# Reordered order strings in a one-core attention and S4 kernel

## The chip, the core and the metric

The kernel runs on one core of a Trainium2 chip, in one launch. The core has five engines that run side by side, each with its own queue of instructions, taken in order: TensorE (PE, matrix multiplies; weight loads are listed as PEld), VectorE (DVE), ScalarE (ACT), GpSimd (POOL) and SyncE (SP, which here only issues DMA transfers). They work on SBUF and PSUM, the on-chip memories; PE writes only PSUM, and a PSUM tile must be read out ("evicted") by DVE or ACT before it can be used again. An instruction that needs another engine's result waits on a semaphore, and everything behind it in its own queue waits too. The metric is the time of one execution on the device in microseconds (us); lower is better.

## The reference

The input `x` has 2048 rows of 512 values in bfloat16. Four layers follow each other: attention (A), S4 convolution (B), A again, B again, each added to its layer-normalised input:

```python
x = A_x
x = x + _A_ref(_layernorm(x, axis=-1), A_wqkv, A_wo)
x = x + _B_ref(_layernorm(x, axis=-1), B_A_re, B_A_im, ...)
x = x + _A_ref(_layernorm(x, axis=-1), A_wqkv, A_wo)
x = x + _B_ref(_layernorm(x, axis=-1), B_A_re, B_A_im, ...)
```

A is sliding-window attention with 32 heads of width 16: row s sees the eight rows s, s−2, ..., s−14. Logits, softmax over the eight, a weighted sum of values and an output projection:

```python
idx = pos[:, None] - off[None, :]          # off = 0, 2, ..., 14
logits = jnp.einsum("bhsd,bhswd->bhsw", q, kg) * scale
attn = _softmax(jnp.where(mask, logits, -1e9), axis=-1)
o = jnp.einsum("bhsw,bhswd->bhsd", attn, vg)
```

B builds, for each of the 512 channels, a convolution kernel of length 2048 from 128 complex modes, `K = sum over n of C exp(dt A l) dt B`, transforms kernel and input with a Fourier transform of length 4096, multiplies, transforms back, and adds `u * Dskip`. The convolution kernel is the same in both B layers.

## The kernel before

Rows stand in 16 blocks of 128, so a block fills the 128 partitions. The work runs through these stages, in the order of time of the profile:

1. **Kernel generation** (`k_gen`, 0 to 107 us). Powers of the modes are built from squares (ACT, L1095, L1113, L1119) and products (DVE, L1099, L1102, L1127), and PE multiplies them into the convolution kernel (L1285). The front of the first attention (layer norm, transposes, projections) is woven in.
2. **First attention** (`LayerA.core`, about 107 to 182). Per quarter of four row blocks and feature tile, DVE multiplies queries with shifted keys (`mult`, L342, tile `prod`), PE sums over the head (`lsum`, L350), DVE takes a maximum (`mx`, L414), ACT exponentials (L430, L453), PE projects values (`v_proj`, L398, evicted at L400). Then, for each of the 16 row blocks, DVE multiplies attention with values (`pv_mult`, L472, tile `pav`), PE sums (L497), ACT evicts (L499) and PE projects out (L508), with ACT adding to x (L512, L514). Layer-norm statistics of the finished rows follow (ACT sums L145, DVE L170, L172, L177, L185, with a power function on POOL, L178, or on ACT, L155 and L156). The normalised rows are then written by DVE (L197) or ACT (L195).
3. **First convolution** (`FftB`, about 182 to 240). PE multiplies by transform matrices in two steps, for the kernel (`K`, then `k`) and for the input (`U`, then `u`). Each result passes PSUM and is evicted by ACT or DVE (`evac`, L810, or L877). DVE multiplies the spectra (`u_mult`, L865, tile `t`). The kernel's spectrum goes through DRAM (tile `kf_dram`) for use in the second convolution. The inverse transform has two steps: `i1` (L891, L895, tile `z`, evicted at L810), and the outputs (`i2` L919 to L926, `i2_cols` L940 to L945, tile `x_sb`). The second step uses the inverse twiddle matrices, `fb.g2` (tile `g_sb`, 1 MB, loaded by SP at L1499).
4. **Front of the second attention** (about 230 to 266), woven into the end of the convolution: layer norm (`h`, `a`, `p`, `n`), transposes on PE (`T`, L271) evicted to `xnT` (`E`, L273), key and query projections (`P`, L282, evicted at L285 to `kT_ext`; `Q`, L223, evicted at L225), and copies that extend the keys over block borders (`x`, `e`, L295).
5. **Second attention** to about 344, **second convolution** to the end, with the stored kernel spectrum read back.

What sets the order of the work is not a planner but strings in the source. For DVE, ACT, PE and SP a program issues the instructions in the order in which the characters of a string call the functions above, and each engine's queue gets its instructions in that order. There are seven:

- `ORDERK`: kernel generation and the front of the first attention.
- `CORE0`, `CORE1`: the two attention cores. `m` is a `prod` multiply, `l` its sum, `q` and `v` projections, `x` maximum, `e` exponentials, `r` reciprocal, `n` normalising of the attention weights, `T` its transposition, `P` and `S` (or `V`) the weighted sum, `O` output projection, `t` statistics, `b` and `d` the beginning and end of a layer norm, `a` and `f` its application to one row block, on DVE and ACT respectively.
- `ORDER0`, `ORDER1`: the two convolutions, with the letters above. `y` is `i1`, `w`, `v` and `z` are outputs; the letter A or D behind a token tells whether ACT or DVE evicts. `g` asks for the inverse twiddle.
- `ORDERF`: the front of the second attention.
- In `CORE1`, capital letters before the rest call the last parts of that front (`RKEYS` names them; `RROWS` gives the engine of each). `KROWS` gives the engine of the eight copies that permute the convolution kernel (L1468, tile `k_perm`).

How a string is run, here for the core:

```python
for c in "".join(order.split()):
    if c in ev:
        ev[c]()
    else:
        next(ops[c])()
```

The functions that the diff touches:

Of the kernel before, what the change touches and what calls it, by code (L numbers as in the profile page):

```python
# [21 lines left out]
S = 2048  # L22
# [20 lines left out]
DQT = 8  # L43
NQT = DQG // DQT
ORDERK = """
iCsCaibCiCbMsiGMisbisCMiibbCMsaiibcMTMMbcisGibbscbGMTibTiTsMbTbTciibTMasTaGcTGaGMaGaiiMMTGGGMlaG
MMsbTMlTWalayyiMaiMybysMiteMateMaMqMMMMaaMqikkQMMKMwMMkMqblMdMTHkqaKlaqQUWUqTaQlUTkkkKayqUUqaypp
aUxaUpyUyxUtkUtpadUeHlKUTTUqeqQkTxkaQKxUkTlkWqTqpK3Tlx3ypkxQTkTpEpyqyy3H3KqkttTQlekWkeTKxUkKUxTU
kkkKkTkUlkKzUzTUTqzUzpUpUUUtKxpeUtUqUExUQepkkUUxxkUKUpEpokxXkUKkoKkkxpKpZXoxXxZZ
"""  # L50
ORDER0 = """
g KD KA KA KA KA KD KD KA KA KD KA kD KA KD KA KD kA UA UD KA UD kA UD UA kD UA UD UA kA kD u kD u m
m u u kA kD u kD UA UA m UA m u UD u kD UA UA m m m u UA kA kD UA kA m kD kA u yD u u m YD u m m m
YA yA u u u m u YA w000A YA m m m yD YA YA yA yD yA w010D yA
"""
LATE0 = "a s t g r b m"
ORDERF = """
yD h01 yA YA v100A v101A h00 v110A v111A h10 a0 v103D p0 n0D v113A h11 z03A S a1 z12A T0 E01D E00A
p1 z02A n1G P02 H2 Q00 P01 T1 a2 E10A p2 P03 E11D P10 P00 n2G H3 P12 a3 T2 E20A p3 P13 E21D n3D P23
P11 P21 T3 E30D P20 E31D x1D P22  # L60
"""
ORDER1 = """
UD UA UA UD UA UD UA UD UA UA UD u UD u u UA m m m UA UD u u u m m m UA u m u u u m u m m u YD m m
YA YA u yA u YD m m u w001A m u YA YA m YA w000D yA yA w010D YA w011D yA yD yA yD yA v102D v100A
v112D v110D v113D v103D v101A v111A
"""

CORE0 = """
mmvvvvlcvvmvllxemvmqrlmcnvlcxqTqvlcvvmmevvvvPqlr1qlPmnql4VTmmqO3lxSPq62lOS57mPlePSmOrSlPnOSPO8xT
SPbeOSrOPSnOPSTOPP9SbdOSPfdOPSOSaaPPfOFSfAOSfabWWWWODtGtCEHfB  # L70
"""
CORE1 = """
DACBFGEJIvHmKmllLN0123qmvqvmlvqmllvvmxvvqlqmemlqrlmnvqTvxmevllvPqvvvmvmqPlrlnmxqqTmSleqSmlPrOSOP
PmSnOSPPTOlblSOSPOxSedPOOrPSbnSPfdPOSWWWWfPOSOPSfPOSafOSbPdOafaStatafOf
"""
ROWS0 = (0, 2, 1, 3, 4, 5, 6, 7, 8, 9, 10, 11, 12, 13, 14, 15)
ROWS1 = (0, 2, 1, 3, 4, 5, 6, 7, 8, 9, 10, 11, 12, 13, 14, 15)
# [1 line left out]
ENGK = dict(b="AAAAAAAAAAAAAAAAA", y="AAAAAAAAAAAA", z="AAAA", e="AAAAAAAA", K="AAAAAAAAAAAAAAAA", Q="AAAAAAAA", x="AAAAAAAAAAAAAAAA")  # L79
STATD = (3,)  # L80
RKEYS = "ABCDEFGHIJKLN"
RROWS = "AADDAADAAADDA"
KROWS = "DDDDDADD"
VROWS = (*range(0, 16, 2), *range(1, 16, 2))


# [1309 lines left out]
def kernel(  # L1396
# [69 lines left out]
    def k_part(h, j):  # L1466
        cp = nc.scalar.copy if KROWS[h * 4 + j] == "A" else nc.vector.tensor_copy
        cp(kp[:, h * 64 + j * 16:h * 64 + (j + 1) * 16, :, :],  # L1468
           krs[h][:, :, j * 64:(j + 1) * 64].rearrange("p a (q r) -> p q a r", r=4))
# [79 lines left out]
    def ring_loads(*ns):  # L1549
        for n in ns:  # L1550
# [6 lines left out]
            ("P", 3, 3), ("Q", 0, 3), ("e", 1), ("e", 2), ("e", 3))  # L1557
    for c, e, (op, *ix) in zip(RKEYS, RROWS, rest):
        ev[c] = lambda e=e, op=op, ix=ix: front[op](*ix, dict(A="act", D="dve")[e])
# [51 lines left out]
```

## Time and profile before

| what | us |
|---|---|
| median of 3 runs | 392.2 |
| runs | 392.21, 392.2, 390.96 |
| the profiled execution, whole | 390.13 |
| its span | 388.4 |
| DVE busy | 369.8 (95%) |
| ACT busy | 336.1 (87%) |
| PE busy | 319.6 (82%) |
| POOL busy | 68.2 (18%) |

The span runs from the first to the last instruction of the trace; some 1.7 us of the execution lie around it. Every number of a row or a stage below is from this one execution, which is 2.1 us shorter than the median of the runs. The granted TensorE clock was 1.00 throughout. In a row of the timeline, the first number is the start in us, the second the duration, then the engine, the line, the operation, the tile written and the tiles read; a bracket at the end tells how long the engine stood idle before it and for whom.

### The profile page before, as it was taken

The numbers are of one execution on the slowest core, as the hardware profiler recorded it, in microseconds if no ns is written. First come the engines' busy times: TensorE is split into PE (matmuls) and PEld (weight loads), VectorE is DVE, ScalarE is ACT, GpSimd is POOL, SyncE is SP. The second block draws the span as 40 slices with busy tenths as digits, with TensorE's granted clock in tenths as the row PEclk, the third lists the DMA queues.
The fourth block names the chain that finished last, engine by engine and source line by source line (L and its number), as shares of the span: only waits on it lengthen the run. The fifth ranks groups of instructions, "written<-read, shape, count | busy, mean of one in ns | idle before, by whom it ended". The sixth has DMA issues, their size and how long they took to land.

```text
span 388.4 us, 14497 instructions
## 1 busy us (share of the span) xinstructions
PE 319.6 (82%) x6312; PEld 219.9 (57%) x6361; DVE 369.8 (95%) x442; ACT 336.1 (87%) x578; POOL 68.2 (18%) x97
## 2 busy tenths in 40 slices
PE   3000178889999998999998999999999998987895
PEld 2000036557634455666887899553445666667895
DVE  6999999999999999999999989979999999989985
ACT  7999999898669799999999998865576779989994
POOL 9400990000190000301622200300000030000000
PEclk9999999999999999999999999999999999999999
DMA  7950730414026465477676734067303076504606
GB/s 202 403 176 17 84 78 2 109 28 98 14 71 189 123 190 146 117 211 236 216 285 236 273 112 111 3 238 251 95 0 95 5 230 210 164 5 123 208 25 196
DMA packets 68301, 54.15 MB, mean 139 GB/s; under 512 B 33545, under 2 KB 58670, under 8 KB 67982
## 3 DMA queue, kind: packets, MB, share of 16 engines
q1 hardware_dynamic: 66566, 48.70, 42.5%
q0 software_dynamic: 1664, 4.52, 3.2%
q8 instruction: 49, 0.80, 0.8%
q14 instruction: 14, 0.11, 0.1%
q10 hardware_dynamic: 8, 0.00, 0.0%
HBM read 30.15 MB, written 13.24 MB: 112 GB/s over the span
## 4 chain that ended last, share of the span: by engine, by line
PE 41%; ACT 17%; DVE 8%; issue 5%; DMA 1%; DVEq 0%; ACTq 0%
PE pq L398 7%; PE pq L223 5%; DVE pav L472 4%; PE pp L282 4%; ACT a1s L810 3%; ACT ub L877 3%; PE po L497 3%; PE L L350 3%; PE pq L508 2%; PE pb L891 2%; PE pb L821 2%; PE pb L895 2%; PE pb L940 2%; PE L L424 2%; PE pb L941 1%
## 5 line engine op out<-in xcount | busy, mean ns | idle before, releaser
L472 DVE TENSOR_TENSOR pav<-attn,v_ext 128x4096 bf16<-128x4096 bf16 (+1 forms) x34 | 72.1, 2158 | 0.0
L342 DVE TENSOR_TENSOR prod<-qT,kT_ext 128x4096 bf16<-128x4096 bf16 x29 | 65.6, 2287 | 1.6 <-ACT qT L225 0.5
L1213 PE MATMUL pt<-ident,x_blk 128*128 128x128 bf16 x64 | 6.0, 242 | 39.3 <-ACT x_blk L195 39.3
L1127 DVE TENSOR_TENSOR A_t<-A_t,pow_t 128x1024 bf16<-128x1024 bf16 (+4 forms) x46 | 37.9, 868 | 0.1
L497 PEld LDWEIGHTS <-pav 64*128 64x128 bf16 x1984 | 30.8, 95 | 11.7 <-DVE pav L472 4.3
L497 PE MATMUL po<-ident,pav 64*128 64x64 bf16 x1984 | 34.3, 190 | 0.2
L508 PE MATMUL pq<-wop,oT 128*128 128x512 bf16 x122 | 31.7, 379 | 3.0 <-issue 2.4
L877 ACT CAST ub<-pb 128x1024 bf16<-128x1024 f32 x32 | 31.7, 1116 | 0.0
L828 PE MATMUL pb<-a1s,w_sb 128*128 128x64 bf16 x768 | 27.7, 193 | 3.6 <-ACT a1s L810 1.9
L810 ACT CAST a1s<-pb 128x1024 bf16<-128x1024 f32 x30 | 29.4, 1054 | 1.4 <-PE pb L821 1.3
L398 PE MATMUL pq<-wv,xnT 128*128 128x512 bf16 x122 | 30.1, 379 | 0.3
L1223 PE MATMUL pp<-xnT,kT_ext 128*128 128x512 bf16 x89 | 25.0, 402 | 5.1 <-ACT xnT L1216 2.0
L400 ACT CAST v_ext<-pq 128x512 bf16<-128x512 f32 x32 | 18.8, 590 | 11.0 <-PE pq L398 11.0
L828 PEld LDWEIGHTS <-w_sb 128*128 128x128 bf16 x768 | 24.9, 98 | 6.0 <-issue 4.3
L1213 PEld LDWEIGHTS <-x_blk 128*128 128x128 bf16 x64 | 4.5, 108 | 40.8 <-ACT x_blk L195 40.1
L178 POOL TENSOR_TENSOR ln_rstd<-ln_rstd,ln_mh 128x4 f32<-128x4 f32 x2 | 6.0, 2984 | 108.7 <-DVE ln_rstd L177 66.1
L1285 PE MATMUL pk<-B_t,A_t 128*64 128x84 bf16 (+1 forms) x512 | 23.4, 201 | 0.7 <-DVE A_t L1127 0.7
L223 PE MATMUL pq<-xnT,kT_ext 128*128 128x512 bf16 x89 | 23.7, 380 | 0.3
L1285 PEld LDWEIGHTS <-A_t 128*64 128x64 bf16 (+1 forms) x512 | 21.5, 103 | 3.9 <-DVE A_t L1127 0.9
L810 DVE CAST a1s<-pb 128x1024 bf16<-128x1024 f32 x18 | 21.4, 1216 | 1.3 <-PE pb L821 1.0
L398 PEld LDWEIGHTS <-xnT 128*128 128x128 bf16 x128 | 12.0, 98 | 15.7 <-issue 2.3
L508 PEld LDWEIGHTS <-oT 128*128 128x128 bf16 x128 | 12.5, 98 | 12.4
(262 smaller groups left out, 896.8 us busy)
## 6 DMA issues: line engine op xcount, KB each, us to landing
w_sb<-w_dram SPq DMA_DIRECT2D x64, 128.0 KB, 3.1
w_dram<-xnT SPq DMA_DIRECT2D x1, 4096.0 KB
kf_ring<-kf_dram SPq DMA_DIRECT2D x13, 256.0 KB, 3.8
kf_ring<-kf_dram SPq DMA_DIRECT2D x26, 128.0 KB, 4.0
v_ext<-v_ext SPq DMA_DIRECT2D x4, 784.0 KB, 5.9
x_blk<-in_A_x_dram SPq DMA_DIRECT2D x4, 512.0 KB, 5.0
kT_ext<-in_A_wqkv_dram SPq DMA_DIRECT2D x4, 512.0 KB, 13.3
x_sb<-in_A_x_dram SPq DMA_DIRECT2D x4, 512.0 KB, 6.8
```

The costliest lines, as they stand in the source:

```text
L223: nc.tensor.matmul(pq[:], lhsT=self.wqk[:, dt, ft * P:(ft + 1) * P], rhs=self.xnT[:, dt, q * 512:(q + 1) * 512], start=(dt == 0), stop=(dt ...
L342: nc.vector.tensor_tensor(pr, self.qT[q][:, ft].unsqueeze(1).to_broadcast([P, W, 4, P]), kap, ALU.mult)
L398: nc.tensor.matmul(pp[:], lhsT=xnT[:, dt, a * P:(a + 1) * P], rhs=wv[:, dt, :], start=(dt == 0), stop=(dt == NDT - 1))
L472: nc.vector.tensor_tensor(pv[:, i], attn[:, n % 4].unsqueeze(2).to_broadcast([P, W, DH // parts, H]), vap, ALU.mult)
L497: nc.tensor.matmul(po[:, h, 0, i * nt + ft, :], lhsT=pvf[rows, i, w, ft * P:(ft + 1) * P], rhs=ident[rows, rows], start=(w == 0 and ft + i ...
L508: nc.tensor.matmul(pw[:], lhsT=oT[:, ftp, :], rhs=self.wo[:, ftp, :], start=False, stop=(ftp == NDT - 1))
L810: (self.nc.scalar.copy if eng == "act" else self.nc.vector.tensor_copy)(dst, src)
L828: nc.tensor.matmul(p2[:, j, :], lhsT=self.w2[:, ec * EC + j, :], rhs=a1s[:, ec * EC + j, :], start=True, stop=True)
L877: nc.scalar.copy(ub[:], p2)
L1127: return lambda: nc.vector.tensor_tensor(*args)
L1223: nc.tensor.matmul(pps[kind, b, ft][:], lhsT=la.wqk[:, dt, c:c + P], rhs=la.xnT[:, dt, b * 512:(b + 1) * 512], start=(dt == 0), stop=(dt = ...
L1285: nc.tensor.matmul(o, lhsT=lhs, rhs=Bt[:, ri, c * CH + ql].rearrange("p b g -> p (b g)"), start=(not half and j % 4 == 0 and ri == 0), sto ...
```

## The change

All seven strings are permuted: the same functions are called, at other places. A few letters change besides. In `CORE0` and in `CORE1` one `a` becomes an `f`. In `ORDER0` one `kA` becomes `kD`; the eight inverse-transform evictions of ACT and DVE (`YA`, `yA`, `YD`, `yD`) become 4, 6, 2, 1 where they were 5, 4, 1, 3; and `g` stands no longer at the head of the string but behind 42 other tokens, ahead of the third `m`. In `ORDERF`, `E20A` becomes `E20D`. In `RROWS` the entry of key L (an extension slice of the keys) goes from D to A, and in `KROWS` the entries of parts E and F change places. `ORDERK` and `ORDER1` hold the same letters as before, in another order.

```diff
 ORDERK = """
-iCsCaibCiCbMsiGMisbisCMiibbCMsaiibcMTMMbcisGibbscbGMTibTiTsMbTbTciibTMasTaGcTGaGMaGaiiMMTGGGMlaG
-MMsbTMlTWalayyiMaiMybysMiteMateMaMqMMMMaaMqikkQMMKMwMMkMqblMdMTHkqaKlaqQUWUqTaQlUTkkkKayqUUqaypp
-aUxaUpyUyxUtkUtpadUeHlKUTTUqeqQkTxkaQKxUkTlkWqTqpK3Tlx3ypkxQTkTpEpyqyy3H3KqkttTQlekWkeTKxUkKUxTU
-kkkKkTkUlkKzUzTUTqzUzpUpUUUtKxpeUtUqUExUQepkkUUxxkUKUpEpokxXkUKkoKkkxpKpZXoxXxZZ
+iCsbCiGsbCaiCiCisGbMisbCMibMMiMGisbTiGbsMbMciibsbbMiisTMbTiGiTbbGMccsTiTaGacGaMGMMiaTbaMMGMMaisl
+GMaiMlTWaTMibaMlwMMTyyyyaMMTMMtseMiateaMMbkqaMkMTqKMMqMQqMaqHUcUladUlQUUTqakWaUQalkUykKUkykkyyTt
+atKUqqeTaaUpapxKpkUUelUxaQkpkdlHUTKxT3qxqWkpKTx3QTlpypTx3Tqpk3qlTkyyTHyWQUtqUTtqKeEkUeQTlTkkzkUK
+UkzKTkKUzTkUzqUTkqtKUktkxpxQpEUexekKUkpxxUkEUkpUKUKkoUxUUkpxopkKkUXKUXpxopXZZxxZ
 """
 ORDER0 = """
-g KD KA KA KA KA KD KD KA KA KD KA kD KA KD KA KD kA UA UD KA UD kA UD UA kD UA UD UA kA kD u kD u m
-m u u kA kD u kD UA UA m UA m u UD u kD UA UA m m m u UA kA kD UA kA m kD kA u yD u u m YD u m m m
-YA yA u u u m u YA w000A YA m m m yD YA YA yA yD yA w010D yA
+KD KA KA KA KA KD KD KA KA KD KA kD kA kD KA KD KA UA KD UA UD KA UD UA kD UA UD UA kA kD u kD u kA
+m UA m u kD UA kD u UA g m UA u m UA UD UD u u m kD m m kA UA u u u kA m kD kA kD m yA u u m m YA YD
+m u yA u m u u m YA YA m m yA YD w000A YA yD yA yA w010D yA
 """
 ORDERF = """
-yD h01 yA YA v100A v101A h00 v110A v111A h10 a0 v103D p0 n0D v113A h11 z03A S a1 z12A T0 E01D E00A
-p1 z02A n1G P02 H2 Q00 P01 T1 a2 E10A p2 P03 E11D P10 P00 n2G H3 P12 a3 T2 E20A p3 P13 E21D n3D P23
-P11 P21 T3 E30D P20 E31D x1D P22
+yD yA YA v101A v100A v110A v113A h01 h00 h10 a0 p0 v103D v111A n0D z03A h11 a1 S z12A T0 E00A E01D
+p1 z02A n1G H2 Q00 a2 P02 P03 T1 E10A E11D p2 P01 P12 n2G P10 H3 P13 T2 a3 p3 P00 E21D P11 E20D P20
+n3D P21 T3 E30D P22 P23 x1D E31D
 """
 ORDER1 = """
-UD UA UA UD UA UD UA UD UA UA UD u UD u u UA m m m UA UD u u u m m m UA u m u u u m u m m u YD m m
-YA YA u yA u YD m m u w001A m u YA YA m YA w000D yA yA w010D YA w011D yA yD yA yD yA v102D v100A
+UD UA UA UD UA UD UA UD UA UA UD u UD u u m u m UA u m UA u m UA m UD u m m u m u u u m m u YA YD u
+YA yA m m YD m u m u m w001A u YA YA m YA w000D yA yA w010D YA w011D yA yD yA yD yA v102D v100A
 v112D v110D v113D v103D v101A v111A
 """
 
 CORE0 = """
-mmvvvvlcvvmvllxemvmqrlmcnvlcxqTqvlcvvmmevvvvPqlr1qlPmnql4VTmmqO3lxSPq62lOS57mPlePSmOrSlPnOSPO8xT
-SPbeOSrOPSnOPSTOPP9SbdOSPfdOPSOSaaPPfOFSfAOSfabWWWWODtGtCEHfB
+vvvmcvlmvvxlcmvelmqvrlcqmnqlmcTxvvlvmvvvmvvqePPl1qmrlnq4lV5mxTqmS3llP2OSP7mqOSeOlPPSr6OmnSOPlbxP
+TdSeOPfrSOPSnOS8TOPSbPAOPSPfW9OSPOSffPOdSEOSfFWBWCfHWDtOGabta
 """
 CORE1 = """
-DACBFGEJIvHmKmllLN0123qmvqmvlqmllvvmxvvqlqmemlqrlmnvqTvxmevllvPqvvvmvmqPlrlnmxqqTmSleqSmlPrOSOP
-PmSnOSPPTOlblSOSPOxSedPOOrPSbnSPfdPOSWWWWfPOSOPSfPOSafOSbPdOafaStatafOf
+CDABIEGFLHvmlKqN0123JmmvllmvqmvvllqvvvqmmxlmleqmqrlnmvqTxvvvePllvvqvvmPqrlnqmlmmTxqSllSmePOPqrSm
+nPOSlWOOSPblWTxPSedPWOrSfOPSfPOSOPSnOSPbOSPWdfOPaSPOSfbPdOaStfOfSfatafO
 """
...
-RROWS = "AADDAADAAADDA"
-KROWS = "DDDDDADD"
+RROWS = "AADDAADAAADAA"
+KROWS = "DDDDADDD"
```

More of the change, by code (lines that the diff above doesn't have):

```diff
@@ L68 @@
 CORE0 = """
-mmvvvvlcvvmvllxemvmqrlmcnvlcxqTqvlcvvmmevvvvPqlr1qlPmnql4VTmmqO3lxSPq62lOS57mPlePSmOrSlPnOSPO8xT
-SPbeOSrOPSnOPSTOPP9SbdOSPfdOPSOSaaPPfOFSfAOSfabWWWWODtGtCEHfB
+vvvmcvlmvvxlcmvelmqvrlcqmnqlmcTxvvlvmvvvmvvqePPl1qmrlnq4lV5mxTqmS3llP2OSP7mqOSeOlPPSr6OmnSOPlbxP
+TdSeOPfrSOPSnOS8TOPSbPAOPSPfW9OSPOSffPOdSEOSfFWBWCfHWDtOGabta
 """
 CORE1 = """
-DACBFGEJIvHmKmllLN0123qmvqvmlvqmllvvmxvvqlqmemlqrlmnvqTvxmevllvPqvvvmvmqPlrlnmxqqTmSleqSmlPrOSOP
-PmSnOSPPTOlblSOSPOxSedPOOrPSbnSPfdPOSWWWWfPOSOPSfPOSafOSbPdOafaStatafOf
+CDABIEGFLHvmlKqN0123JmmvllmvqmvvllqvvvqmmxlmleqmqrlnmvqTxvvvePllvvqvvmPqrlnqmlmmTxqSllSmePOPqrSm
+nPOSlWOOSPblWTxPSedPWOrSfOPSfPOSOPSnOSPbOSPWdfOPaSPOSfbPdOaStfOfSfatafO
 """
```

## The prediction

> **What bounds the kernel now.** I read the page's span, engine shares and end chain first, then busy time by stage, then what VectorE (DVE) waits for, then single rows where the diff moves something.
>
> ```profile
> span 388.4 us, 14497 instructions
> ...
> PE 319.6 (82%) x6312; PEld 219.9 (57%) x6361; DVE 369.8 (95%) x442; ACT 336.1 (87%) x578; POOL 68.2 (18%) x97
> ...
> PE 41%; ACT 17%; DVE 8%; issue 5%; DMA 1%; DVEq 0%; ACTq 0%
> ```
> ```profile
> 160.00:170.00 10.00, 9.52 (x286) 6.33 (x289) 9.90 (x9) 9.80 (x26) 1.97 (x1) 1.00 0.68 197
> 170.00:182.00 12.00, 11.35 (x311) 7.27 (x316) 11.90 (x21) 11.82 (x27) 0.00 (x0) 1.00 0.70 214
> ...
> 200.00:220.00 20.00, 17.16 (x506) 15.98 (x504) 20.00 (x19) 20.00 (x23) 5.56 (x11) 1.00 0.77 285
> ...
> 230.00:258.00 28.00, 27.89 (x372) 20.13 (x367) 24.90 (x68) 22.37 (x39) 3.50 (x4) 1.00 0.22 65
> 258.00:300.00 42.00, 41.53 (x365) 18.84 (x370) 40.87 (x24) 26.58 (x44) 0.00 (x0) 1.00 0.43 141
> ```
> ```profile
> DVE x_sb L943 <- PE pb L941: 1.8, 4, 0.8
> ...
> DVE xnT L273 <- PE pt L271: 1.3, 1, 1.3
> DVE z L810 <- PE pb L895: 1.1, 1, 1.1
> DVE a1s L810 <- PE pb L821: 1.0, 2, 0.8
> ...
> DVE kT_ext L295 <- ACT kT_ext L285: 0.9, 1, 0.9
> DVE ln_nb L185 <- ACT ln_rstd L156: 0.7, 2, 0.5
> DVE prod L342 <- ACT qT L225: 0.5, 1, 0.5
> ```
>
> In the second fence the columns after the window's length are busy time of PE, weight load, DVE, ACT and POOL, then clock, DMA share and GB/s. DVE is idle for only 388.4 − 369.8 = 18.6 us. In the first convolution (200 to 220) DVE and ACT are both busy all 20.00 us; in the front of the second attention (230 to 258) PE is full (27.89 of 28), and after it (258 to 300) PE and DVE together (41.53 and 40.87 of 42). The chain names PE most, but an order earns only where it fills a hole, and the holes are small: the waits of the third fence sum to 7.3 us, of which 1.8 (x_sb) lie in the last convolution's tail, whose tokens keep their order. So 5.5 us is the most that these waits can yield, and since most are waits on a full PE, I expect a fraction.
>
> **Work that changes engine.** These durations price it:
>
> ```profile
> L197 DVE TENSOR_SCALAR xnT<-x_sb,ln_rstd,ln_nb 128x512 bf16<-128x512 bf16 x11 | 4.3, 415 | 0.1
> ...
> L273 DVE COPY xnT<-pt 128x1024 bf16<-128x1024 bf16 x5 | 3.2, 662 | 1.3 <-PE pt L271 1.3
> ...
> L295 DVE COPY kT_ext<-kT_ext 128x508 bf16<-128x508 bf16 x4 | 1.1, 285 | 0.0
> ```
> ```profile
> L195 ACT ACTIVATE xnT<-x_sb,ln_nb,ln_rstd 128x512 bf16<-128x512 bf16 x13 | 10.6, 814 | 0.0
> ...
> L273 ACT COPY xnT<-pt 128x1024 bf16<-128x1024 bf16 x3 | 3.1, 1018 | 0.0
> ...
> L295 ACT COPY kT_ext<-kT_ext 128x508 bf16<-128x508 bf16 x4 | 2.5, 621 | 0.1
> ```
>
> Each attention core moves one normalisation from DVE to ACT (CORE0, CORE1: one `a` becomes `f`): DVE −2 × 0.415, ACT +2 × 0.814. `E20` goes ACT to DVE: DVE +0.662, ACT −1.018. The slice `L` goes DVE to ACT: −0.285, +0.621. In ORDER0 one `k` eviction goes to DVE and one inverse-transform eviction comes back: of like size, zero. The two swapped permuted copies are zero too. Sum: DVE −0.83 + 0.66 − 0.29 = −0.45 us, ACT +1.63 − 1.02 + 0.62 = +1.23 us over the span. That alone moves nothing by more than a tenth of a per cent; what counts is where the holes go. I therefore took the changed order of each engine and added up row durations of the same instructions, stage by stage, letting each wait for its producer.
>
> **Kernel generation, 0 to 107.** DVE is full here, and the new order separates some pairs in which a DVE instruction needs the one right before it.
>
> ```profile
> 46.09 0.68 DVE L1127 TENSOR_TENSOR B_t<-B_t 128x1024 bf16<-128x1024 bf16 x1
> 46.69 0.68 DVE L1127 TENSOR_TENSOR cm_t<-B_t 128x1024 bf16<-128x1024 bf16 x1
> ...
> 64.95 0.69 DVE L1127 TENSOR_TENSOR A_t<-A_t,A_t 128x1024 bf16<-128x1024 bf16 x1
> 65.67 1.23 DVE L1127 TENSOR_TENSOR A_t<-A_t,pow_t 128x2048 bf16<-128x2048 bf16 x1
> ...
> 107.24 2.29 DVE L342 TENSOR_TENSOR prod<-qT,kT_ext 128x4096 bf16<-128x4096 bf16 x1 [0.51 <-PE L L350]
> ```
>
> Independent neighbours overlap: 46.69 − 46.09 = 0.60 for an instruction of 0.68. A dependent pair does not: 65.67 − 64.95 = 0.72 for 0.69. That is some 0.11 us a pair, and of eight such pairs at L1127 four remain: −0.46. Against it, two of the new A_t/B_t positions come before ACT's squares are done, by 0.28 and 0.2 in my sums: +0.3 to +0.5, estimated. I take −0.2 (bounds −0.5 and +0.3). [...] The stage's end (prod at 107.24, waiting 0.51 for PE) has the same order of work ahead of it in both, so part of either sign can still disappear there.
>
> **First attention and the hand-over to the first convolution, 107 to 183.**
>
> ```profile
> L178 POOL TENSOR_TENSOR ln_rstd<-ln_rstd,ln_mh 128x4 f32<-128x4 f32 x2 | 6.0, 2984 | 108.7 <-DVE ln_rstd L177 66.1
> ```
> ```profile
> 154.91 1.20 DVE L414 TENSOR_REDUCE mx<-L 128x128 bf16<-128x1024 f32 x1
> ...
> 158.77 8.90 DVE L472 TENSOR_TENSOR pav<-attn,v_ext 128x4096 bf16<-128x4096 bf16 x4
> ```
> ```profile
> 182.31 2.84 ACT L810 CAST a1s<-pb 128x1024 bf16<-128x1024 f32 x3
> ```
>
> POOL's power of 2.98 us stands between L177 and ln_nb, and DVE goes on with other work meanwhile. Before, four multiplies (8.90 us) cover it; after, a maximum and one multiply, 1.20 + 8.90 / 4 = 3.4 us, so it is covered with 0.4 to spare and costs nothing. If that cover fails, DVE stands with all its multiplies queued behind ln_nb: up to 1 us, by the maximum's slot. The extra ACT normalisation falls at about 160, where ACT is idle only 0.20 + 0.18 us until 182 (second fence): 0.81 − 0.38 = 0.4 of it comes out late at ACT's first eviction (182.31). A variance step (L172) that moves up waits up to 0.5 for ACT's sums. DVE itself would arrive 0.35 earlier. PE and both evictors start the convolution together, so I charge the later one: +0.4, bounds −0.35 and +0.75.
>
> **First convolution, 182 to 240.** Both evictors are full, so a kf eviction or multiply earlier or later changes only who waits; ACT's and DVE's sums differ from before by under 0.15 us. The hole before the inverse transform (1.1 in the third fence) is DVE waiting for PE while ACT still has its queue of evictions; it shrinks only if ACT is earlier, and it isn't. I take −0.1, bounds −0.5 and +0.5. The load `g`:
>
> ```profile
> 183.96 1.54 SPq L1499 DMA_DIRECT2D g_sb<-g_dram  x1
> ...
> 200.07 5.82 SPq L853 DMA_DIRECT2D kf_nat<-kf_nat  x8
> ```
> ```profile
> g_sb<-g_dram SPq DMA_DIRECT2D x1, 1024.0 KB, 6.0
> ```
> ```profile
> 226.11 1.19 ACT L945 CAST x_sb<-pb 128x1024 bf16<-128x1024 f32 x1
> ```
>
> It is issued at 183.96 and lands 6.0 us later. After, it is issued by SP between the transfers around 205, behind which eight quarter swaps of 3.6 us are in line, and lands by 215 even if it takes 10; the first output that needs it is evicted at 226.11. SP has no other work there that DVE waits on within 5 us. Cost zero; if the swaps behind it are late by its whole 6.0 us, 1 us reaches DVE.
>
> **Front of the second attention, 240 to 266.**
>
> ```profile
> 254.30 1.29 DVE L273 COPY xnT<-pt 128x1024 bf16<-128x1024 bf16 x2 [1.27 <-PE pt L271]
> ...
> 257.09 1.23 DVE L295 COPY kT_ext<-kT_ext 128x2032 bf16<-128x2032 bf16 x3 [0.90 <-ACT kT_ext L285]
> 258.36 2.29 DVE L342 TENSOR_TENSOR prod<-qT,kT_ext 128x4096 bf16<-128x4096 bf16 x1
> ...
> 264.00 4.49 DVE L342 TENSOR_TENSOR prod<-qT,kT_ext 128x4096 bf16<-128x4096 bf16 x2 [0.55 <-ACT qT L225]
> ```
>
> The 1.27 stays: PE is full, and as many matmul groups stand ahead of the last transposition. Of the three extension copies that now follow it (1.23 together, 0.4 each) one, `x0`, is asked for ahead of the one that waits, so it lies in the 0.90, and the first prod starts 0.3 to 0.4 earlier, the 0.3 because its other slice still waits for ACT's eviction of `P30`. Q01 becomes the fifth group instead of the third, but slice `L` on ACT removes the 0.55. Fourth prod: 266.05 against 266.20. I take −0.3 (bounds 0 and −1.0).
>
> **Rest of the second attention and its end, 266 to 346.**
>
> ```profile
> 299.15 2.29 DVE L342 TENSOR_TENSOR prod<-qT,kT_ext 128x4096 bf16<-128x4096 bf16 x1 [0.28 <-issue]
> ...
> 342.19 0.16 DVE L185 SCALAR_TENSOR_TENSOR ln_nb<-ln_ag,ln_rstd 128x3 f32<-128x3 f32 x1 [0.53 <-ACT ln_rstd L156]
> ```
>
> The 0.28 falls away in my sums: −0.2 beyond the front. At the end CORE1 puts ACT's normalisations ahead of an output eviction that used to stand in front of them, so ACT reaches the last rstd about 0.4 earlier, which takes most of the 0.53; the eviction put back comes 0.25 later, and PE, which needs both, starts the second convolution 0.4 earlier. I take −0.4; the bounds are 0 (PE waits for the eviction instead) and −0.8 (the 0.53 and the 0.28 of the next wait both go). Second convolution: same pace and same tail, +0.1.
>
> **Sum.** −0.2 + 0.4 − 0.1 − 0.3 − 0.2 − 0.4 + 0.1 = −0.7 us. The profiled execution took 390.13 (span 388.4 and 1.7 around it), so 389.4. It is 2.1 under the shown median of 392.2; the same step from that median gives 391.5.
>
> **Rivals.** (a) Faster: ACT's late arrival is hidden, because DVE's earlier evictions already free PE, and the convolution's hole shrinks with it: −0.5 (generation) − 0.35 (hand-over) − 0.5 (convolution) − 0.3 − 0.2 (second attention) − 0.4 (its end) + 0.1 = −2.15, so 390.0. For it: DVE has less to do and fewer dependent pairs. Against: PE is full from 230 to 300, and no order makes it shorter.
> (b) Slower: ACT becomes the bound at the hand-over and stays behind through the first convolution. It enters 0.75 + 0.5 late, and since DVE, ACT and PE share one ring of PSUM tiles there, a late eviction stops the others; two missed slots of one ACT eviction each (2.84 / 3 = 0.95) add 1.9. With the other gains (0.7 + 0.4 = 1.1) that is 1.25 + 1.9 − 1.1 = +2.05: 394.25. It decides once the lag goes beyond 1.1 + 1.2 = 2.3 us, the gains and the bound of measurement. For it: 20.00 of 20.00 on both engines, no slack to recover; against: ACT's totals there hardly move.
> (c) No change, because PE's full stretch absorbs whatever comes before 230 and the rest offsets: it is my forecast's neighbour, 392.2.
>
> **How the numbers follow.** A change under 0.3% (1.2 us) can hardly be told from none. My sum and (c) lie inside it: 0.37. (a), faster: 0.36. (b), slower: 0.27. The forecast's own range is 391.0 to 392.9, from the stage bounds taken half each. The range, 389.2 to 394.7, goes past (a) by 0.8, since the front's bound (−1.0) lies beyond what (a) uses, and past (b) by 0.4, and leaves out about one in ten on each side.
>
> **What would show it.** In the profile after: ACT's first L810 eviction at 182.7 instead of 182.31 and no DVE wait over 0.5 at L172 or L185 before it; the 1.1 for z L810 still there; no wait on g_sb at L940; kT_ext L295 down to 0.6 or less, prod on qT gone; the 0.28 at 299 gone; ln_nb L185 under 0.3. It is wrong if DVE waits on POOL's power, if DVE or ACT shows holes between 185 and 228, or if PE waits for a group between 240 and 300 that was ready before.

## The result and the profile after

22 executions of each kernel were compared: a median of 391.14 us before and of 392.50 us after, a ratio of 1.0035 with a 95% interval of 1.0022 to 1.0049. The change makes the kernel slower by 1.36 us. The forecast was 391.5 and no measurable change, with a small gain behind it; the time lies in the stated range, the sign does not.

The page of the profile after (span, engines, end chain), in the columns of the page before:

```profile
span 392.6 us, 14546 instructions
...
PE 327.3 (83%) x6361; PEld 222.0 (57%) x6361; DVE 369.7 (94%) x440; ACT 337.1 (86%) x580; POOL 63.4 (16%) x97
...
PE 39%; ACT 16%; DVE 6%; issue 4%; DMA 4%; SPq 3%; DVEq 0%; ACTq 0%
```

The work is what was counted: DVE is busy 369.7 us against 369.8, ACT 337.1 against 336.1. The span is 4.2 us longer all the same, so the time went into holes. That is more than the 1.36 us of the medians, because of which executions were profiled: the one after took 394.37 us, the slowest of its 22, and the one before 390.13, a little under the fastest of its 22 (390.24). What DVE waits for, in total, times and longest:

```profile
DVE x_sb L943 <- PE pb L941: 2.8, 4, 1.3
...
DVE pav L472 <- ACT ln_junk L145: 1.4, 1, 1.4
DVE prod L342 <- PE L L350: 1.3, 2, 0.8
...
DVE kf_nat L810 <- PE pb L828: 1.0, 1, 1.0
DVE xnT L273 <- PE pt L271: 0.9, 1, 0.9
...
DVE kT_ext L295 <- ACT kT_ext L285: 0.7, 2, 0.6
DVE z L810 <- PE pb L895: 0.7, 1, 0.7
DVE prod L342 <- ACT qT L225: 0.6, 1, 0.6
DVE ln_bn L138 <- PE pq L508: 0.6, 2, 0.4
```

Three of these matter below, new or grown: kf_nat (1.0, in the first convolution), x_sb (1.8 before, 2.8 after) and pav (1.4, in the second attention). PE is behind the first two. Its own rows there, and one at 316 ahead of the third, in the timeline of PE and of its weight loads:

```profile
197.27 0.22 PE L821 MATMUL pb<-F1c,xnT 128*64 128x128 bf16 x1 [0.91 <-issue]
...
231.78 0.10 PEld L941 LDWEIGHTS <-g_sb 128*128 128x128 bf16 x1 [0.52 <-issue]
...
316.18 0.54 PE L497 MATMUL po<-ident,pav 64*128 64x64 bf16 x14 [0.84 <-issue]
```

"issue" says that PE waited for nothing that the profile shows: no producer was late. In the trace before there is no such stop over 0.2 us between 150 and 340. I use the word stop for these rows below.

To see the stages, I read four rows of the DVE timeline in each run: the first prod of the first attention, the first eviction of each convolution, and the first prod of the second attention. All in us:

| kernel | first prod | convolution 1 starts | from there to the second attention's first prod | from there to convolution 2 | from there to the end |
|---|---|---|---|---|---|
| before | 107.24 | 181.98 | 76.38 | 86.14 | 43.86 |
| after | 106.93 | 181.53 | 78.07 | 88.13 | 44.88 |

The first two columns gained 0.31 and 0.45, as far as the end of the first attention. Then the first convolution and the front lose 1.69, the second attention 1.99, and the last stage 1.02. One execution is one draw, and this one was the slowest, so the experiments decide which of these belong to the change. The last column can be set aside at once: DVE's last outputs start 380.86 before and 384.08 after, so the span's end follows 7.5 us behind them before and 8.5 after, and the runs below with the same second convolution have 43.8.

### The profile page after: what moved, and what is told of

It is laid out like the page before. It is cut to its first block, busy times and chain, and to the rows that moved or that the text cites. A ratio compares the mean times of both kernels' runs of the same rounds, so it can differ in the third digit from the quotient of the medians.

```text
span 392.6 us, 14546 instructions
## 1 busy us (share of the span) xinstructions
PE 327.3 (83%) x6361; PEld 222.0 (57%) x6361; DVE 369.7 (94%) x440; ACT 337.1 (86%) x580; POOL 63.4 (16%) x97
## 4 chain that ended last, share of the span: by engine, by line
PE 39%; ACT 16%; DVE 6%; issue 4%; DMA 4%; SPq 3%; DVEq 0%; ACTq 0%
PE pq L398 7%; PE pq L223 5%; PE pp L282 4%; ACT ub L877 3%; PE po L497 3%; PE L L350 3%; ACT a1s L810 3%; PE pq L508 2%; DVE t L865 2%; SPq L1390 2%; DMA w_sb<-w_dram 2%; PE pb L891 2%; PE pb L895 2%; PE L L424 2%; PE pb L940 2%
## 5 line engine op out<-in xcount | busy, mean ns | idle before, releaser
L508 PE MATMUL pq<-wop,oT 128*128 128x512 bf16 x128 | 33.7, 385 | 0.1
L877 ACT CAST ub<-pb 128x1024 bf16<-128x1024 f32 x32 | 32.5, 1124 | 0.0
L1223 PE MATMUL pp<-xnT,kT_ext 128*128 128x512 bf16 x96 | 26.8, 410 | 4.9 <-ACT qT L1228 2.1
L1213 PEld LDWEIGHTS <-x_blk 128*128 128x128 bf16 x64 | 5.4, 118 | 41.8 <-ACT x_blk L195 40.6
L499 ACT CAST oT<-po 128x512 bf16<-128x512 f32 x31 | 17.8, 574 | 4.3 <-PE po L497 4.3
```

Of the source, the lines that this page charges most:

```text
L508: nc.tensor.matmul(pw[:], lhsT=oT[:, ftp, :], rhs=self.wo[:, ftp, :], start=False, stop=(ftp == NDT - 1))
L877: nc.scalar.copy(ub[:], p2)
L1223: nc.tensor.matmul(pps[kind, b, ft][:], lhsT=la.wqk[:, dt, c:c + P], rhs=la.xnT[:, dt, b * 512:(b + 1) * 512], start=(dt == 0), stop=(dt = ...
```

## The experiments

**Which strings.** Four mixtures of the two kernels. The label names what is new in the kernel before, or old in the changed one.

```diff
-ORDER0 of before
+ORDER0 of the change, in the kernel before
```


> Kernel before with ORDER0 of the change alone (order of the first convolution, late g, the swapped evictions). Theory 1, the loss sits in the order of the first convolution: slower than before by 0.9 to 1.4 us, ratio 1.002 to 1.004. Theory 2, the loss comes from the order of the second attention: within 0.3 us of before. Theory 3, it comes from stops of PE that no producer explains (three in the profile after, 1.04, 0.52 and 0.96 us) and that belong to single executions, not to an order: within 0.5 us of before, and the profile has such stops at other places or none.

Measured: 392.67 us, ratio 1.0035 (1.0022 to 1.0048). The first convolution's order alone gives the whole loss. In the profiled execution the stage from the convolution's start to the second attention's first prod takes 78.39 us, 2.01 more than before, and both of its stops are there again, together 1.56:

```profile
197.79 0.22 PE L821 MATMUL pb<-F1c,xnT 128*64 128x128 bf16 x1 [0.62 <-issue]
...
232.77 0.22 PE L940 MATMUL pb<-xnT,g_sb 128*128 128x128 bf16 x1 [0.94 <-issue]
```

A third stop (0.65 at 145.64) lies in the first attention, whose order is that of the kernel before. So a stop alone does not tell that an order is at fault.

```diff
-ORDERF, CORE1, RROWS of before
+ORDERF, CORE1, RROWS of the change, in the kernel before
```


> Kernel before with ORDERF, CORE1 and the one letter of RROWS of the change (front and core of the second attention). Theory 1: within 0.3 us of before, or faster by up to 0.7 us as predicted. Theory 2: slower by 0.9 to 1.5 us, ratio 1.002 to 1.004. Theory 3: within 0.5 us.

Measured: 390.78 us, ratio 0.9999 (0.9978 to 1.0019). The second attention's order costs nothing on the whole.

```diff
-ORDERK, CORE0, KROWS of before
+ORDERK, CORE0, KROWS of the change, in the kernel before
```


> Kernel before with ORDERK, CORE0 and KROWS of the change (kernel generation and first attention). All theories: faster by 0.3 us, since both milestones, the first prod and the first eviction of the convolution, come 0.3 us earlier in the profile after; if what is gained there is lost again in the full first convolution, within 0.2 us.

Measured: 390.70 us, ratio 0.9988 (0.9971 to 1.0005); first prod at 106.91, convolution 1 at 181.49. It looks like the expected gain, but the interval takes in no change.

```diff
-ORDER0 of the change
+ORDER0 of before, in the changed kernel
```


> Changed kernel with ORDER0 of before put back. Theory 1: the loss is gone, within 0.4 us of before or faster. Theory 2: the loss stays, slower than before by about 1.2 us. Theory 3: between, with PE stops or a lowered clock in the profile only by chance.

Measured: 391.30 us, ratio 1.0004 (0.9987 to 1.0021). The loss is gone. Theory 1 holds: the loss sits in the first convolution's order. But a stop is left here too, in the second attention:

```profile
314.71 0.58 PE L497 MATMUL po<-ident,pav 64*128 64x64 bf16 x28 [0.86 <-issue]
```

**What the stops are.** I counted PE's instructions (weight loads, multiplies and some twenty semaphore instructions) from the start of the trace. In the runs whose PE records are complete, the stops lie at numbers 5058 and 6850 (changed kernel, e1) and 9154 (changed kernel, e2, e4): the same numbers in different runs, and 7 and 9 times 256 apart. Part 3 of the page has a queue for instructions (`q8 instruction: 50, 0.82, 0.9%` after), whose packets in the trace have 16384 bytes each. After has 50 such packets for PE's 12742 instructions, one for 255 on average. Every 256th number from 194 on takes in all three stops, and in the profile after each packet starts between 1.7 us before and 2.9 us after PE comes to one of these numbers. My reading of these figures is that PE's instructions arrive here in blocks of 256, and that a stop stands where a new block begins. For each stop of the changed kernel, and the same block in e3 (which has the old ORDER0 and CORE1), the time at which PE entered the block before, the packet's start and landing, PE's next instruction, and how long PE was at work on the block before (us):

```
kernel   enters block   packet starts   lands     PE goes on   stop   block takes
after    192.17         194.98          195.93    197.27       0.91   4.2
e3       192.12         192.78          194.14    196.19       none   4.1
after    227.82         229.31          230.46    231.78       0.40   3.6
e3       226.56         227.36          228.49    230.15       none   3.6
after    312.22         313.30          314.70    316.18       0.84   3.1
e3       308.99         310.10          310.98    313.17       none   4.2
```

No row shows when a packet is asked for. In e3, without stops at these places, it starts 0.66, 0.80 and 1.10 us after the block before is entered, so my estimate is that it is asked for at about that entry. At the stops PE goes on 1.32 to 1.48 us after it has landed, and in the profile after PE enters no block sooner than that. At 192 the old order leaves the packet 0.7 us late, the new one 2.8 us. The third stop is of another kind: its packet starts no later than in e3 (1.08 us after the block is entered, against 1.10; it then takes 1.40 against 0.88), but with the new CORE1 PE is through the block in 3.1 us instead of 4.2. The busy tenths of the DMA engines from 190 to 200, in 40 slices of 0.25 us, first after and then in e3:

```profile
DMA  0019699799989999999930000000006979884200
```
```profile
DMA  0029798970069699970000399897728789883059
```

After, the engines are busy at 6 tenths or more from 190.75 to 195; in e3 there is a hole at 192.25 to 192.75, at whose end the packet starts (192.78). The evictions of the second and third kernel spectra stand next to each other in the new order (`kD kA kD`), and their swaps and stores to DRAM were asked for closer together: the four swaps of these two start at 190.80 to 193.04 after, at 191.78 to 195.05 in e3. This was the theory (A) that the next runs tested; B is that g's late load itself costs, C that the new evictions do.

```diff
-KD KA KA ... kD u UA g m UA ...
+g KD KA KA ... kD u UA m UA ...
```


> Changed kernel with g put back to the head of ORDER0, nothing else. Theory A, PE runs out of instructions: its stops lie at every 256th instruction of its stream, when the DMA that brings the next 16 KB of instructions had to stand behind data transfers. The stop at 197 us stays (0.6 to 0.9), since the two kn transfers in a row that cause it stay; the one at 232 (0.4 to 0.9) goes, since without g among the swaps the weights of the next attention are asked for earlier. So 0.4 to 0.9 us faster than the changed kernel, ratio to before 1.001 to 1.002. Theory B, the late load itself costs, because its data are late or it delays the swaps: the whole loss of the first convolution goes, ratio 1.000.

Measured: 393.01 us, ratio 1.0060 (1.0037 to 1.0084): not faster than the changed kernel, if anything slower. The stop at 197 stayed (0.84), but the one at 232 did not go, it grew (1.21). So B falls: late g is not what costs. My reason for expecting the second stop to go falls too, since the key weights (1 MB) were asked for at 225.5, later than in the changed kernel (224.7). The stop itself fits A: the shorter the time from asking for the weights to PE's entry into the block (3.8 us in e3, 3.1 after, 2.6 in e1, 2.2 in e5), the later the packet started (0.8, 1.5, 2.1 and 2.4 us after the entry) and the longer the stop (none, 0.40, 0.94 and 1.21).

```diff
         T = {name: turned_by(...) for name in ("B_re", "B_im", "C_re", "C_im")}
+        extra = pst.tile([P, 4, P], F32, name="pt")
+        for _ in range(48):
+            nc.tensor.matmul(extra[:, 0, :], lhsT=ident[:], rhs=ident[:], start=True, stop=True)
```


> Changed kernel with 48 matrix multiplies more (96 PE instructions with their weight loads) at about 8 us, where PE is idle until 40; no order, wait or transfer is changed, only the places of the 256-instruction blocks. Theory A: the stops at 197, 232 and 316 are gone, because the blocks now end elsewhere; 0.9 to 1.8 us faster than the changed kernel, ratio to before 0.999 to 1.001. Theory C, the holes belong to the new order of evictions (who evicts when): nothing changes, ratio 1.0035.

Measured: 392.79 us, ratio 1.0049 (1.0030 to 1.0067). The stops at 197, 232 and 316 are gone, as A says, but others came (the largest 0.58 at 230.62, 0.59 at 167.80, 0.81 at 234.35 and 0.87 at 384). A had told that the old places would be freed, not that new ones would be hit as hard. The gain is not there.

The same 48 multiplies in the kernel before, and 64 in the changed kernel with the old ORDER0:

> Kernel before with the same 48 matrix multiplies. Theory A: stops may come up at other places (the first outputs of the first convolution, about 229, are the likeliest: the block before them is then reached at 225, with the key weights' transfer under way until 227), up to 0.8 us slower, ratio 1.000 to 1.002. Theory C: within 0.2 us of before.

> Changed kernel with the old ORDER0 and 64 matrix multiplies more at 8 us (128 instructions). Theory A: the stop at 315 (0.86) of the run with the old ORDER0 goes, no stop of over 0.4 comes up; 0.8 us faster than that run, ratio to before 0.997 to 0.999. Theory C: no change, 1.0004.

Measured: 396.07 us, ratio 1.0111 (1.0080 to 1.0143), and 391.99 us, ratio 1.0028 (1.0012 to 1.0044). Both are slower. 48 multiplies at 8 us, where PE has nothing to do for 30 us, cost the kernel before 4.9 us in the medians, though the order of its own work is not changed. Its PE has this row, and its DVE this wait, from 180 to 262:

```profile
193.66 0.37 PE L828 MATMUL pb<-a1s,w_sb 128*128 128x64 bf16 x4 [2.70 <-issue]
```
```profile
DVE a1s L810 <- PE pb L821: 4.0, 2, 3.8
```

PE entered the block before at 186.42, while the 1 MB of g was under way, issued at 184.55:

```profile
g_sb<-g_dram SPq DMA_DIRECT2D x1, 1024.0 KB, 7.3
```

The last number is the time to landing, so it was under way until 191.9. The engines were not full all that time, as their busy tenths from 184 to 194 show, in 40 slices of 0.25 us:

```profile
DMA  8998889912689999896110000000979989200000
```

From 188.75 to 191.0 they are at 0 or 1. The packet started at 191.29, landed at 192.24, and PE went on 1.42 later. What held it while the engines were almost idle, no view here shows. In e8 the stop at 315 went, and stops came at 190.68 (0.55) and 381.89 (0.92). The clock was lower from 15 to 60 in these runs (0.52 and 0.66 in e6), but the first prod came at 106.95 in e6 and 106.93 in e8, so that cost nothing by then. C falls: it had said no change.

A fourth shift, which I had picked by laying the blocks over the transfers of the changed kernel's trace:

```diff
-        for _ in range(48):
+        for _ in range(32):
```


> Changed kernel with 32 matrix multiplies more (64 PE instructions) at 8 us. Theory A: every 256-instruction block ends 64 instructions earlier. Read against the transfers in the trace of the changed kernel, none of the three places of stops is hit any more, and no new one before 380 but a small one near 143, where PE has slack; ratio to before 0.997 to 1.001. If the holes belong to the order of evictions, ratio 1.0035 and holes at 197 and 232 as before.

Measured: 394.09 us, ratio 1.0079 (1.0061 to 1.0097). The pick failed: stops at other places (1.09 at 238.06 the largest). I take it that the transfers moved too, with PE; at any rate the places of the stops in e10 could not be read off the trace of the changed kernel.

**Taking the cause away, and adding it.** First, one token, to leave the DMA a hole at 192:

```diff
-... KA kD kA kD KA KD KA UA ...
+... KA kD kA KA KD KA kD UA ...
```


> Changed kernel with one token of ORDER0 moved: the third k eviction stands three evictions later, as far behind the second as in the kernel before (kD kA KA KD KA kD where the change has kD kA kD KA KD KA). Theory A: the stop at 197 comes from the transfers of the second and third kernel spectra, which the change asks for in one go, just as PE enters the block whose successor has to be fetched; apart, they leave the instruction fetch a hole, the stop at 197 shrinks under 0.3, DVE's wait on kf_nat (1.05) goes, and the time falls by 0.5 to 1.0 us to a ratio of 1.001 to 1.002; the stops at 232 and 316 stay. If the data traffic isn't the cause, the stop stays at 0.6 to 0.9 and so does the ratio, 1.0035.

Measured: the stop at 197 and DVE's wait on kf_nat are gone, as expected, and from the convolution's start to the second attention's first prod this execution took 77.24 against 78.07. But the median is 392.05, ratio 1.0032 (1.0017 to 1.0047). The timed runs do not show the gain.

```diff
 (with the third k as in the run before)
-... u u m YA YA m m yA YD w000A YA yD ...
+... u u m YA w000A YA m m yA YD YA yD ...
```


> Changed kernel with the third k eviction put back as in the run before (three evictions later) and the first output token w000A put back in front of the last two m, as it stands in the kernel before. Theory A: no PE stop at 197; the first output is multiplied by PE 2 to 3 us earlier, so that DVE's wait for its second output (1.0 in the run with k alone, 0.24 before) shrinks under 0.5, and the stage from the convolution's first eviction to the first prod of the second attention takes 76.2 to 76.8 us as before instead of 77.2. Ratio to before 0.999 to 1.001. If the rest of the loss isn't in that place, the stage stays at 77 and the ratio at 1.002 or above.

> The same kernel once more as a second look: a second profiled execution and as many timed runs, to tell what of the stops and stages repeats from execution to execution. Theory A: the same instruction numbers of PE stop, if any (the one at 315), within 0.2 us, and the stage times repeat within 0.3 us; the time outside the stages, the clock and the last stage may differ by 1 us.

The second of these is the same kernel again, whatever its label says. Measured: 392.14 us, 1.0034 (1.0015 to 1.0054), and 391.96 us, 1.0021 (1.0002 to 1.0040). The stage took 77.39 and 76.93. In the first profiled execution PE stopped for 0.48 at 231, in the second it did not stop there; the one at 315 came both times (0.71, 0.67). So the size of a stop differs between executions of one kernel, and my expectation of 1.000 failed.

Then the opposite: traffic added to the kernel before, and nothing else.

```diff
     la = LayerA(tc, nc, consts, lnst, A_wqkv, A_wo, 1, xnT, 1)
     la.front_w()
+    la.front_w()
```


> Kernel before with the load of the second attention's key and query weights (2 transfers of 512 KB at 223 us) asked for twice, the second behind the first; no instruction of PE, DVE or ACT is changed or moved, and the weights are needed only at 242. Theory A: the transfers now fill the DMA engines until about 232 instead of 227.8. PE enters a new block at 226.6 and its successor at 230.2; the fetch of the latter is asked for in the first of these moments and has to stand behind the weights, so PE stops at 230 for 0.5 to 3 us, DVE's wait for its second output (0.24) grows by as much, and the time by 0.5 to 2 us, ratio 1.001 to 1.005. If PE's stops don't come from data traffic, nothing changes: under 0.2 us.

Measured: 392.54 us, ratio 1.0057 (1.0032 to 1.0083). PE's row, and SP's, which ask for the weights twice:

```profile
235.26 0.22 PE L940 MATMUL pb<-z,g_sb 128*128 128x128 bf16 x1 [1.28 <-issue]
```
```profile
223.14 0.39 SPq L254 DMA_DIRECT2D kT_ext<-in_A_wqkv_dram  x1
223.59 0.64 SPq L255 DMA_DIRECT2D kT_ext<-in_A_wqkv_dram  x1
227.12 0.37 SPq L254 DMA_DIRECT2D kT_ext<-in_A_wqkv_dram  x1
228.57 0.37 SPq L255 DMA_DIRECT2D kT_ext<-in_A_wqkv_dram  x1
```

The stop came one block later than I had said. Between the two loads the DMA engines had a hole at 227.75, in which the first packet got through; the next, which by my estimate was asked for at 230.4, started at 232.84 behind the second load, landed at 233.82, and PE went on at 235.26. The stage grew from 76.38 to 77.83, by 1.45. This run shows it without any change of order: with more transfers ahead of PE's next instructions, PE stopped for 1.28 us, and the kernel is slower by 0.57%.

**A version that beats both?**

> The kernel before with the new kernel generation and first attention once more (the run of before was 0.9988, interval 0.9971 to 1.0005), to narrow it: every theory says 0.3 to 0.5 us faster than before, ratio 0.9987 to 0.9993, and in the profile the first prod at 106.9 and the convolution's first eviction at 181.5.

Measured: 390.76 us, ratio 0.9999 (0.9984 to 1.0014). With e3's 0.9988 the new first half is not told from no change. No version here beats both kernels.

## Why the prediction was wrong

**Step that failed: the first convolution.** "A kf eviction or multiply earlier or later changes only who waits", −0.1 with bounds of 0.5 on both sides. It was reckoned with DVE, ACT and PE as three queues whose instructions are always there. By e1 the stage's order alone is worth +1.34 us. It moved the swaps and stores of the kernel spectrum against PE's instruction blocks, and the instructions themselves came late: in e1's profile the stage is 2.01 us longer, with two stops of 0.62 and 0.94. The prediction named the sign of this failure, holes on DVE or ACT between 185 and 228, and they came (the rows at 197.56 and 198.60 below). The row that should have warned me, the instruction queue in part 3 of the page, I had passed over at 0.8% of the DMA time: what counts was not its share but what stands before it.

How much of the 1.34 is stops is not settled. In the profiled executions the stage takes 76.4 to 76.6 with the old ORDER0 (before, e2, e3, e4, e14), 78.1 to 78.8 with the new one (after, e1, e5), and 76.9 to 77.4 with the first stop taken away (e9, e11, e12). But the spans of all executions on record have these quartiles:

```
kernel        executions   lowest   quarter   middle   three quarters
before        110          388.3    388.5     388.9    389.6
e1            12           389.6    390.0     390.4    390.7
e4            12           388.6    389.1     389.5    389.9
after         22           389.2    390.0     390.6    391.4
e9             9           389.2    389.8     390.3    390.6
e11           12           388.7    389.6     390.4    391.0
e12           12           389.1    389.5     390.1    390.7
```

Before comes close to its lowest value in a quarter of its executions, and its profiled one, without stops, is near it (388.4). The changed kernel lies 0.9 higher at its lowest and 1.7 in the middle, and spreads more. e9, e11 and e12 stay 0.6 to 0.9 above e4 in the middle, and their profiled stages 0.3 to 0.8 above e4's 76.60. Whether that is the stop at 231, more often or larger in other executions, or the order itself, no run here tells.

The granted clock of each execution, averaged over it, is on record too, and tells a part. In the changed kernel it was 0.990 to 0.996 in 10 of the 22 executions, and those have a middle span of 391.4; the other 12 have 390.0 (three of them lie at 0.94, as nine of the kernel before do, and are not slower). Of the 110 executions before, one lies there. None of e1's 12 does, so the loss of the first convolution's order is not the clock's. But 3 of 12 in e2 (391.1 against 388.5 for the rest), 6 of 12 in e3 and 7 of 12 in e4 (389.9 against 388.8) do, so the other new orders bring more executions with a lowered clock, which in these runs are the slower ones (in e9 and e12 they are not). No run separates this from the rest of the loss.

**Luck in the time.** The forecast of 391.5 is a step of −0.7 from the median of 3 runs, 392.2; the 22 executions before have 391.14. So the forecast time is only 1.0 off while the forecast change is 2.1 off: a base that was too high hid half of the error. From 391.14 the forecast's own range of 391.0 to 392.9 would be 389.9 to 391.8, which leaves 392.50 out; the wide range would still take it in. And 0.3% was not too small to be seen: the interval of the result is 0.13% to either side.

**Hand-over, +0.4: wrong in sign.** ACT's first eviction came at 181.97, not 182.7 (182.31 before), DVE's at 181.53 (181.98 before). The extra normalisation on ACT was hidden, and POOL's power was covered as said. So rival (b) named the right stage and the right side, but not its mechanism: ACT was not late, and DVE and ACT have their new holes (1.05 and 1.10) at the same moment, behind PE:

```profile
198.60 2.38 DVE L810 CAST kf_nat<-pb 128x1024 bf16<-128x1024 f32 x2 [1.05 <-PE pb L828]
```
```profile
197.56 1.01 ACT L810 CAST a1s<-pb 128x1024 bf16<-128x1024 f32 x1 [1.10 <-PE pb L821]
```

**Kernel generation, −0.2: near.** 0.31 earlier in the profile after, 0.08 to 0.33 in the two runs of that half alone; no timed run resolves it. In e12, whose generation has the same order, the first prod came only at 108.05, and the granted clock was 0.50 from 63 to 66; in e11, the same kernel, the clock stayed at 1.00 there and the first prod came at 106.92.

**Late g, 0: right.** (In the changed string it stands behind 43 other tokens, not 42.) It landed 5.3 us after its issue at 208.69, ahead of the first output, which PE begins at 227.0, and e5 is not better.

**Front, −0.3: not there.** In e2 the stage took 76.36 against 76.38. In the profile after the wait for kT_ext shrank (0.9 to 0.7), but the wait on qT that should have gone is 0.6.

**Second attention and its end, −0.2 − 0.4: there, and taken back.** Where PE does not stop at 315 (e6 and e8, whose blocks lie elsewhere) this stage takes 85.67 against 86.14: −0.47. With the stop (e4) it takes 86.67. The stop at 315 came in every run with the new CORE1 and unshifted blocks, and the gain brings it on: the new order takes PE through that block in 3.1 us, where the old one needs 4.2, and the next instructions are not there yet. In e4 the block was entered at 310.72, the packet went from 311.67 to 313.08 and PE went on at 314.70.

**Second convolution, +0.1: right.** 43.83 to 43.86 in most runs.

Forecast and rival (c) had no change come from gains and losses that offset. What the stages show is gains of about 0.4 and 0.5 us, against stops of PE, and in some executions a lowered clock, that no part of the sum contained.

## What to carry to other kernels

PE ran 12742 small instructions here, and they are in the trace as transfers too: 50 packets of 16384 bytes. In these runs holes on PE with "issue" as releaser stood at the same instruction numbers (5058, 6850, 9154) in several runs, a multiple of 256 apart. Where a trace of another kernel has such holes, look for the packets in the same way: see what DMA traffic is under way when PE enters the block before, and how fast PE is through it (the blocks before the changed kernel's stops took 3.1 to 4.2 us). In this kernel, with DVE busy for 94 to 95% of the span, a change of order that comes to nothing in a sum of durations cost 0.3%, and 48 extra multiplies in idle time 1.1%, so reorderings like these are to be judged by many executions and not by a sum of row durations.

## What the hardware showed that was not expected

PE's granted clock was 0.50 behind some of its stops. In the profiled execution after it was 0.50 from 316.25 to 319.65, for 3.4 us, behind the stop at 316; in e4, with a stop of the same size (0.86) in the same place, it stayed at 1.00. First two windows of the profile after, then the same two of e4:

```profile
315.00:320.00 5.00, 4.16 (x63) 2.18 (x56) 5.00 (x4) 2.37 (x3) 0.75 (x1) 0.66 0.58 172
...
317.00:318.00 1.00, 1.00 (x7) 0.42 (x4) 1.00 (x3) 0.59 (x1) 0.00 (x0) 0.50 0.88 261
```
```profile
315.00:320.00 5.00, 4.97 (x124) 2.99 (x118) 4.98 (x4) 4.50 (x10) 0.00 (x0) 1.00 0.77 230
...
317.00:318.00 1.00, 1.00 (x44) 0.90 (x45) 1.00 (x1) 0.97 (x3) 0.00 (x0) 1.00 0.91 264
```

The clock is the third number from the end. In e2 it fell too:

```profile
315.00:320.00 5.00, 5.00 (x96) 2.81 (x91) 3.58 (x4) 3.11 (x8) 0.00 (x0) 0.69 0.73 211
```

The two executions in which it fell took 88.13 and 87.76 for this stage, e4 86.67. The difference, 1.1 to 1.5 us, is my estimate for the slow clock, and the wait of pav (1.4), which the profiles after and e2 have and e4's does not, goes with it. The stop's length does not tell the two cases apart: the clock fell behind 0.84 us in after and in e2, and did not behind 0.86 in e4. Nor did it fall behind this stop in e5, e9, e11 and e12 (0.81, 0.85, 0.71 and 0.67), nor behind the stop of 1.28 in e13; around the end of e7's stop of 2.70 it did (0.50 from 194 to 196, and 0.77 and 0.87 in the 2 us on either side). What decides between the two is open.

A packet of instructions can wait long. In e7 it started 4.9 us after PE had entered the block before, with the 1 MB load under way, and in the profile after 2.8 us, at the end of a stretch of busy engines. The packets themselves took 0.9 to 1.6 us from start to landing in the profiles before and after. What sets the length of such a delay no trace here tells.
